# Forming the weight sums of a seven-product block scheme on GpSimd instead of VectorE

## Chip, cores, metric

One core of one Trainium2 chip. The time is that of the device, in microseconds (us), of one execution; lower is better. The engines are PE (TensorE matmul) with PEld (its weight loads), DVE (VectorE), ACT (ScalarE), POOL (GpSimd) and SP (SyncE). In the profile a line such as L331 is a line of the kernel. SBUF and PSUM are the two on-chip memories: in this kernel the results of PE's products lie in PSUM, and weights, activations and sums in SBUF.

## The reference

A gated recurrence over 4 sequences of 6080 steps and 256 channels, then a two-layer block with `h - tanh(h)` between its layers (256 to 2048 to 256), on the 24320 resulting rows, all in float32. Shortened:

```python
sig = 1.0 / (1.0 + np.exp(-f_logit))
f = lower_bound + (1.0 - lower_bound) * sig
for t in range(S):
    h = f[:, t] * h + (1 - f[:, t]) * x[:, t]
    y[:, t] = h
...
h = x @ w_in                 # x: y as 24320 rows
g = h - np.tanh(h)
return (g @ w_out).astype(np.float32)
```

## The kernel before

The rows go through in 48 blocks: one of 256 rows, then 47 of 512. From the third block on, both matrix products use a scheme with seven block products in place of eight (Winograd's form of Strassen's). It needs, for each of the four parts of `w_in` and of `w_out`, three sums S1, S2, S4 of weight blocks, and a difference S3, which takes the place of block A21. The sums are formed once and then serve all blocks. The first two blocks are computed plainly (eight products) while the weights, which arrive as 64-bit numbers, are still being rounded to float32 on DVE and ACT.

```python
w_in  = [wpool.tile([P, 7, 2 * P], FP32, name=f"w_in{u}")  for u in range(NU)]   # NU = 4
w_out = [wpool.tile([P, 7, 2 * P], FP32, name=f"w_out{u}") for u in range(NU)]
A11, S3, A12, A22, S1, S2, S4 = range(7)
...
def sum_weight(kind, u, s3):
    w = (w_in, w_out)[kind][u]
    A21 = S3
    sums = (
        (S1, A21, A22, ALU.add),
        (S2, S1, A11, ALU.subtract),
        (S4, A12, S2, ALU.subtract),
    )
    for o, a, b, op in ((S3, A11, A21, ALU.subtract),) if s3 else sums:
        nc.vector.tensor_tensor(
            out=w[:, o, :], in0=w[:, a, :], in1=w[:, b, :], op=op
        )
```

The order of instructions is fixed by hand in a list of words, one queue per engine. `cw.i` is the last step of rounding a weight (L132), `sc` the recurrence (L231, a scan), `F` a plain product of the first layer (L687), `S` one of the second (L754), `A.k.u` the three sums of part u of `w_in` (k=0) or `w_out` (k=1), `B.k.u` its difference. `K1` are filler matmuls.

```python
before = """
    ... cw.1 sc0.1 ... sc1.1 cr.2 K1.2 ... F.1.0.0 ... F.1.0.1 ... cw.2 ... F.0.1.0 ...
    cw.3 ... S.0.0.0 ... cw.4 ... F.0.2.0 ...
    q.0.3.0 A.0.0 F.1.3.0 ... cw.7 ... B.0.0 ... A.0.1 ... B.0.1 ... cw.8 ... A.0.3 ... A.1.3 ... A.0.2 ...
"""
```

## Time and profile before

| | before |
|---|---|
| median of 3 runs | 2330.94 us (2330.39 to 2331.64) |
| PE busy of the 2330.1 us span | 2318.8 us |
| DVE busy | 2121.3 us |
| POOL busy | 0.7 us |
| the 32 sums, on DVE | between 67 and 131 us |

The prediction below shows the page's lines and reads them.

```profile
18.16 0.67 DVE L725 SCALAR_TENSOR_TENSOR q<-q,t 128x512 f32<-128x512 f32 x1
18.75 0.69 DVE L138 TENSOR_SCALAR e<-raw 128x1024 int32<-128x1024 int32 x1
...
30.96 1.43 DVE L132 SCALAR_TENSOR_TENSOR w_out<-r,e 128x256 f32<-128x256 f32 x4
```

### The profile page before, as it was taken

How to read it: one execution, taken by the hardware profiler on the slowest of the kernel's cores; microseconds unless marked ns; L12 is line 12 of the kernel's file. 1: busy time of each engine (PE TensorE's matmuls, PEld its weight loads, DVE VectorE, ACT ScalarE, POOL GpSimd, SP SyncE). 2: the span in 40 equal slices, each digit the busy share in tenths (PEclk: the TensorE clock that was granted, in tenths of full speed). 3: DMA queues.
4: the chain of work that ended last, by engine and by line, in shares of the span. 5: the costliest groups of instructions: out<-in, count | busy, mean ns of one | idle time of the engine just before them, and what ended most of it. 6: DMA issues, size and time to landing. Idle time of an engine off the chain costs nothing.

```text
span 2330.1 us, 28649 instructions
## 1 busy us (share of the span) xinstructions
PE 2318.8 (100%) x10676; PEld 2025.3 (87%) x10676; DVE 2121.3 (91%) x2447; ACT 1800.6 (77%) x2686; POOL 0.7 (0%) x6
## 2 busy tenths in 40 slices
PE   9999999999999999999999999999999999999998
PEld 5888888888888888888888888888888888888887
DVE  8999899998999989999899999999899998999987
ACT  7777777777777777787777777777777777777775
POOL 0000000000000000000000000000000000000000
PEclk9999999999999999999999999999999999999999
DMA  6311211112111111111111121111211112111101
GB/s 172 64 23 29 45 37 28 28 33 41 37 28 28 37 37 37 28 28 40 33 37 28 28 44 30 37 28 28 46 28 37 28 28 46 31 33 28 28 10 29
DMA packets 296948, 85.05 MB, mean 36 GB/s; under 512 B 289888, under 2 KB 292704, under 8 KB 296800
## 3 DMA queue, kind: packets, MB, share of 16 engines
q1 hardware_dynamic: 296512, 82.87, 16.9%
q8 instruction: 85, 1.39, 0.3%
q14 instruction: 63, 0.52, 0.1%
q10 hardware_dynamic: 288, 0.26, 0.0%
HBM read 58.20 MB, written 24.90 MB: 36 GB/s over the span
## 4 chain that ended last, share of the span: by engine, by line
PE 99%; DMA 0%; DVE 0%; issue 0%; ACT 0%; SPq 0%
PE A L388 27%; PE Qd L471 14%; PE Qa L471 14%; PE D L388 14%; PE Qb L471 14%; PE B L388 7%; PE Qc L471 7%; PE A L687 1%; PE Qc L754 1%; PE Qa L754 1%; PE Qb L754 1%; PE D L687 0%; PE Qd L687 0%; PE B L687 0%; DMA fn<-in_f_logit_dram 0%; PE Qa L687 0%
## 5 line engine op out<-in xcount | busy, mean ns | idle before, releaser
L388 PE MATMUL A<-T,w_in 128*128 128x256 f32 x2208 | 558.8, 379 | 0.0
L388 PEld LDWEIGHTS A<-T,w_in 128*128 128x128 f32 x2208 | 419.5, 190 | 57.0
L432 DVE TENSOR_TENSOR h<-h,q 128x1024 f32<-128x1024 f32 x368 | 437.6, 1220 | 3.1
L426 DVE SCALAR_TENSOR_TENSOR q<-q,t 128x1024 f32<-128x1024 f32 x368 | 440.0, 1216 | 0.0
L419 ACT ACTIVATE q<-t 128x1024 f32<-128x1024 f32 x368 | 382.8, 1053 | 46.7 <-DVE h L432 43.8
L416 ACT ACTIVATE t<-h 128x1024 f32<-128x1024 f32 x368 | 388.6, 1056 | 3.1 <-DVE h L403 0.3
L437 ACT ACTIVATE junk<-t 128x1024 bf16<-128x1024 f32 x368 | 388.1, 1055 | 1.5
L451 DVE TENSOR_TENSOR Tg<-h 128x1024 f32<-128x1024 f32 x368 | 348.0, 946 | 6.4
L471 PE MATMUL Qb<-h,w_out 128*128 128x256 f32 x1472 | 347.7, 379 | 0.0
L471 PEld LDWEIGHTS Qb<-h,w_out 128*128 128x128 f32 x1472 | 279.7, 190 | 38.0
L471 PE MATMUL Qd<-h,w_out 128*128 128x256 f32 x736 | 219.0, 379 | 0.0
L471 PE MATMUL Qa<-Tg,w_out 128*128 128x256 f32 x736 | 219.0, 379 | 0.0
L471 PE MATMUL Qa<-h,w_out 128*128 128x256 f32 x736 | 218.9, 379 | 0.0
L471 PE MATMUL Qd<-Tg,w_out 128*128 128x256 f32 x736 | 218.9, 379 | 0.0
L400 ACT COPY h<-B 128x512 f32<-128x512 f32 x184 | 106.9, 581 | 143.0 <-PE B L388 94.2
L400 ACT COPY h<-A 128x512 f32<-128x512 f32 x184 | 107.2, 583 | 136.7 <-PE A L388 125.3
L403 DVE TENSOR_TENSOR h<-D,r 128x512 f32<-128x512 f32 x184 | 126.9, 689 | 92.7 <-PE D L388 89.1
L403 DVE TENSOR_TENSOR h<-A,r 128x512 f32<-128x512 f32 x184 | 126.3, 687 | 73.8 <-PE A L388 42.1
L400 ACT COPY r<-A 128x512 f32<-128x512 f32 x184 | 107.2, 583 | 105.9 <-PE A L388 105.9
L388 PE MATMUL D<-T,w_in 128*128 128x256 f32 x736 | 188.9, 379 | 0.0
L388 PE MATMUL A<-y,w_in 128*128 128x256 f32 x736 | 188.9, 379 | 0.0
L388 PE MATMUL B<-y,w_in 128*128 128x256 f32 x736 | 188.9, 379 | 0.0
(120 smaller groups left out, 3069.2 us busy)
## 6 DMA issues: line engine op xcount, KB each, us to landing
xn<-in_x_dram SPq DMA_DIRECT2D x184, 128.0 KB, 3.3
fn<-in_f_logit_dram SPq DMA_DIRECT2D x184, 128.0 KB, 3.1
out_dram<-osb SPq DMA_DIRECT2D x180, 128.0 KB, 2.8
raw<-in_moe_w_out_dram SPq DMA_DIRECT2D x8, 512.0 KB, 4.9
raw<-in_moe_w_in_dram SPq DMA_DIRECT2D x7, 512.0 KB, 4.7
out_dram<-osb SPq DMA_DIRECT2D x3, 256.0 KB, 3.9
fn<-in_f_logit_dram SPq DMA_DIRECT2D x1, 512.0 KB, 7.3
xn<-in_x_dram SPq DMA_DIRECT2D x1, 512.0 KB, 8.2
```

Of the source, the lines that this page charges most:

```text
L388: nc.tensor.matmul(ps[:, c], lhsT=w_in[u][:, slot, c * P : (c + 1) * P], rhs=mixes[j][right], start=start and c == 0, stop=True, skip_grou ...
L400: nc.scalar.copy(out=dst, in_=piece(n, bank))
L403: nc.vector.tensor_tensor(out=piece(n, "h")[:, q], in0=piece(n, bank), in1=piece(n, r), op=ALU.add)
L416: nc.scalar.activation(out=half(n, i, "t"), in_=half(n, i), func=AF.Square)
L419: nc.scalar.activation(out=half(n, i, "q"), in_=half(n, i, "t"), func=AF.Square, scale=RA, bias=RB,)
L426: nc.vector.scalar_tensor_tensor(out=q, in0=q, scalar=RC, in1=t, op0=ALU.add, op1=ALU.mult)
L432: nc.vector.tensor_tensor(out=h, in0=h, in1=q, op=ALU.mult)
L437: nc.scalar.activation(out=junk[:, :, :, 0 : st[n]["hb"]], in_=t, func=AF.Relu, bias=-TINY, accum_out=flags[:, 2 * n + i : 2 * n + i + 1],)
L451: nc.vector.tensor_tensor(out=o, in0=a, in1=b, op=ALU.subtract)
L471: nc.tensor.matmul(acc[j, part][:, r, 0 : st[n]["hb"]], lhsT=w_out[u][:, slot, c * P : (c + 1) * P], rhs=piece(n, right)[:, q, c], start=( ...
L687: nc.tensor.matmul(h[c], lhsT=w_in[u][:, 2 * k + s, c * P : (c + 1) * P], rhs=ys[j][:, k, 0:nb], start=k == 0 and (c == 0 or len(banks) == 2),
L754: nc.tensor.matmul(acc[j][i // 2][:, i % 2].rearrange("p (k m) -> p k m", k=2), lhsT=plain[j, u][:, s, c, i * P : (i + 1) * P], rhs=w_out[ ...
```

## The change

The intent: DVE is 91% busy and GpSimd idle, so the sums of the weights move to GpSimd, in the same order.

```diff
@@ -328,7 +328,7 @@
             for o, a, b, op in ((S3, A11, A21, ALU.subtract),) if s3 else sums:
-                nc.vector.tensor_tensor(
+                nc.gpsimd.tensor_tensor(
                     out=w[:, o, :], in0=w[:, a, :], in1=w[:, b, :], op=op
                 )
```

## The prediction

> **What bounds the kernel now.** I read four views in this order. First the page of the profile: busy time by engine, and the chain that ended last.
>
> ```profile
> PE 2318.8 (100%) x10676; PEld 2025.3 (87%) x10676; DVE 2121.3 (91%) x2447; ACT 1800.6 (77%) x2686; POOL 0.7 (0%) x6
> ...
> PE 99%; DMA 0%; DVE 0%; issue 0%; ACT 0%; SPq 0%
> ```
>
> PE (TensorE) is busy 2318.8 of 2330.1 us and the chain that ended last is PE for 99%; GpSimd (POOL) is empty. Next the busy time in stretches that I chose round the changed work.
>
> ```profile
> core 0: us, PE busy (x) PEld busy (x) DVE busy (x) ACT busy (x) POOL busy (x), PEclk, DMA share, GB/s
> 0.00:20.00 20.00, 14.76 (x60) 9.65 (x61) 13.11 (x24) 11.73 (x23) 0.70 (x6) 0.91 0.98 268
> 20.00:67.00 47.00, 47.00 (x174) 32.85 (x173) 46.45 (x63) 37.80 (x60) 0.00 (x0) 1.00 0.42 121
> 67.00:131.00 64.00, 64.00 (x282) 53.24 (x282) 58.62 (x94) 46.69 (x76) 0.00 (x0) 1.00 0.24 46
> ...
> 200.00:2200.00 2000.00, 2000.00 (x9269) 1760.61 (x9268) 1830.99 (x2076) 1560.67 (x2317) 0.00 (x0) 1.00 0.16 33
> 2200.00:2331.00 131.00, 123.99 (x578) 108.39 (x576) 108.33 (x124) 89.96 (x134) 0.00 (x0) 0.99 0.07 17
> ```
>
> All of PE's idle time lies in the first 20 us (5.2) and the last stretch (7.0). From 20 us on it has no hole. DVE (VectorE) is also nearly full from 20 to 67 us, 46.45 of 47. Third, the changed line by itself.
>
> ```profile
> L331 DVE TENSOR_TENSOR w_in<-w_in x16: 389/424/430, 67.3 to 119.1; 128x256 f32<-128x256 f32 x16
> L331 DVE TENSOR_TENSOR w_out<-w_out x16: 416/422/427, 97.4 to 130.2; 128x256 f32<-128x256 f32 x16
> ```
>
> There are 32 of them in the whole kernel, all between 67 and 131 us, where PE waits for nothing. Last, the timelines of DVE and PE in the opening (columns: start, length, then the work), for how close DVE runs ahead of PE.
>
> ```profile
> 15.19 0.68 DVE L132 SCALAR_TENSOR_TENSOR w_in<-r,e 128x512 f32<-128x512 f32 x1
> 15.79 2.45 DVE L231 TENSOR_TENSOR_SCAN y<-f,y,v 128x512 f32<-128x512 f32 x2
> ...
> 23.42 1.22 DVE L132 SCALAR_TENSOR_TENSOR w_in<-r,e 128x1024 f32<-128x1024 f32 x1
> ...
> 40.52 1.22 DVE L132 SCALAR_TENSOR_TENSOR w_in<-r,e 128x1024 f32<-128x1024 f32 x1
> ```
>
> ```profile
> 18.39 0.59 PE L858 MATMUL B<-zeros 128*128 128x512 bf16 x2
> 18.82 1.88 PE L687 MATMUL Qa<-y,w_in 128*128 128x512 f32 x4
> ...
> 25.69 1.89 PE L687 MATMUL B<-y,w_in 128*128 128x256 f32 x8
> ...
> 42.91 1.89 PE L687 MATMUL D<-y,w_in 128*128 128x256 f32 x8
> ```
>
> The scans end at 18.24 and PE uses their y at 18.82, after filler matmuls: 0.6 us of slack. The second weight block is rounded by 24.64 and used at 25.69: 1.05 us. The third is ready at 41.74 and used at 42.91: 1.2 us. These are DVE's tightest dates; bank releases and second-layer weights have 2 us and more.
>
> **What the Trainium skill says.** "GPSIMD Engine Reference", section 3.1, gives a two-input tensor_tensor as about 2.6 cycles an element, 4497 ns for 2048 fp32 columns, about twice VectorE. No GpSimd tensor_tensor is in this trace to compare; the DVE rows here, 424 ns for 256 columns, 688 for 512 and 1220 for 1024, are about 1.04 ns an element, consistent with its VectorE figure (2293 ns). "SBUF — State Buffer", section "Who interferes with whom": a VectorE instruction with two SBUF inputs, or in a two-port mode, and a GpSimd instruction that reads SBUF exclude each other for a whole instruction, the later one waiting. The trace before can't show it, having no such GpSimd work. "Perfetto Trace Analysis", section "Optimizing Scalar/DVE Operations", warns for that reason that moving work between the two "might not help".
>
> **The change part by part.**
> *Removed from DVE:* eight groups of three dependent sums and eight single differences. In the timeline a triple takes 1.25 us of queue (67.29 to 68.54) and a single 0.34 (82.07 to 82.41): 8 x 1.25 + 8 x 0.34 = 12.7 us, all after 67 us. None is on the path that sets the end, since PE has no hole there. Worth: 0.
>
> *Added to GpSimd:* 32 instructions of 256 columns. Estimate from the page's 4497 ns: 4497 x 256 / 2048 = 0.56 us, plus dispatch, say 0.65 us; within a triple each waits for the one before, say 0.2 us more. In all some 32 x 0.85 = 27 us of an empty engine, spread over about 110 us. PE needs them in time: the first (S1 of the first block) at 89.7 us, the last group at 140 to 157. Enough.
>
> *Moved:* order is kept per engine, but GpSimd has nothing ahead of the sums, so each now starts when its operands are ready instead of in its place in DVE's queue. By the instruction order built from the changed kernel, the first triple waits only for the rounding that ends at 15.87 us, so it runs from 16 us instead of 67; the first difference waits for PE's plain products of that block (about 25.7 us); the second triple for the rounding at 24.64; its difference for PE at about 43 us; the triple of the fourth block for the rounding at 60.8. So eight GpSimd sums land between 16 and 45 us, where DVE has no slack time and its results are used within 0.6 to 1.2 us. The other 21 come after the last rounding (96.2 us), where DVE is relieved of its sums and starts with two transposes and waits for PE.
>
> *What that costs if the page's lock is as it says and the two alternate* (each sum holds DVE up for its 0.65 us unless DVE is on an instruction with a PSUM input). First sum asked for at 16.1, granted at 17.0 between the scans: y late by 0.65 against 0.6 of slack, PE loses about 0.1 to 0.2. Three sums before the second rounding: 3 x 0.65 = 1.95 late less 1.05 of slack: PE is 0.9 to 1.1 behind. Three more (a difference, two sums; the last sum of that triple falls beside a PSUM read) before the third rounding: 6 x 0.65 = 3.9 less 1.2, so PE is about 2.7 behind. After that the dates have 2 us and more of their own beyond this 2.7, and DVE's lead grows by the 12.7 us removed. A delay of PE is never recovered, since it has no idle to give back: about +2.7 us on 2330.9, that is 2333.6.
>
> **The rivals.**
> 1. *Nothing moves.* DVE keeps the port by issuing back to back, and GpSimd fits into PSUM reads (one at 19.95 us, others at 26.9, 29.8, 30.4, 34.0), or the two overlap better than the page says. For: dates for the sums are 45 us off in the early part. Against: the measured lock of the page. Time: 2330.9.
> 2. *GpSimd becomes late itself.* After 96.2 us nine sums lie between the third block's triple and the first second-layer difference, needed at 119.0 us. With each waiting for a 1.2 us DVE instruction, 9 x 1.85 = 17 us from about 101 to 118. Close, but DVE also has holes there (1.2 us at 126 already before). If missed, 1 to 3 us more: 2334 to 2337.
> 3. *Faster, because DVE is relieved at 91% busy.* Against: the sums are not in the 2000 us of steady work at all, and PE has no hole where they were. It could be tenths at most.
>
> **Range and chances.** I give the lock with alternation about half, nothing about 40%, late sums 10%. Between 2330.9 and 2333.6 I choose 2332.5. The low end is the lowest of before; the high end adds 0.9 us a sum instead of 0.65 in the early part (6 x 0.9 - 1.2 = +4.2 and some lateness). Two per cent is 47 us, which nothing here reaches: same 0.985, faster 0.005, slower 0.01.
>
> **What would show it right or wrong.** In the changed kernel's trace: 32 sums on POOL with starts at 16 to 20, 25 to 45, and after 60 us; a start-to-start spacing of 0.7 to 1 us in an undisturbed triple; the second scan, the second rounding and the third rounding later than 18.24, 24.64 and 41.74 by 0.65, 2 and 4 us if the lock holds, unchanged if not; PE holes before the matmuls that stood at 25.69 and 42.91 and nowhere else, of about 1 and 1.7 us; from 200 to 2200 us PE still full. The prediction is wrong if PE waits for POOL anywhere, if a sum on POOL takes well over 1 us, or if the time falls below 2330.

## More of the kernel before

```profile
32.57 3.62 PE L754 MATMUL Qa<-w_out,h 128*128 128x256 f32 x16
```

The columns are start, length (both us), engine, line, operation, what it writes and reads, shapes and count. The four pieces of the rounding start 0.33 us apart; the product reads the first two, done by 31.7, and starts at 32.57.

## The result

| | median, us | runs, us |
|---|---|---|
| before | 2331.29 | 2330.39 to 2331.98 (4) |
| changed | 2332.36 | 2331.95 to 2332.43 (4) |

The ratio is 1.0003, 95% interval 0.9988 to 1.0018: the same within 2%. A ratio here is the mean time of one kernel's fast runs over that of the other's fast runs of the same rounds, so it is not quite the ratio of the medians.

The page and the stretches of the changed kernel, in the forms shown of before:

```profile
PE 2319.1 (100%) x10674; PEld 2024.9 (87%) x10676; DVE 2117.5 (91%) x2415; ACT 1801.5 (77%) x2686; POOL 43.7 (2%) x38
...
PE 98%; DVE 1%; DMA 0%; issue 0%; SPq 0%; ACT 0%; DVEq 0%
```

```profile
20.00:67.00 47.00, 45.47 (x169) 31.56 (x168) 46.84 (x62) 38.33 (x60) 14.63 (x8) 1.00 0.39 120
67.00:131.00 64.00, 63.95 (x281) 53.26 (x281) 53.63 (x63) 46.23 (x75) 24.10 (x21) 1.00 0.23 46
...
200.00:2200.00 2000.00, 2000.00 (x9268) 1760.62 (x9267) 1830.50 (x2076) 1561.18 (x2316) 0.00 (x0) 1.00 0.16 33
```

DVE has 32 instructions fewer and POOL 32 more. The steady 2000 us are untouched. PE lost 1.53 us between 20 and 67 us, where it had no hole before, and DVE now has a share in the chain that ended last. The sums by themselves, and GpSimd's timeline:

```profile
L331 POOL TENSOR_TENSOR w_in<-w_in x16: 730/1056/4455, 15.0 to 117.8; 128x256 f32<-128x256 f32 x16
```

```profile
15.00 4.37 POOL L331 TENSOR_TENSOR w_in<-w_in 128x256 f32<-128x256 f32 x3 [13.69 <-DVE w_in L132]
23.65 9.00 POOL L331 TENSOR_TENSOR w_in<-w_in 128x256 f32<-128x256 f32 x4 [4.28 <-PE Qd L687]
42.88 2.41 POOL L331 TENSOR_TENSOR w_in<-w_in 128x256 f32<-128x256 f32 x1 [10.23 <-PE B L687]
61.43 3.54 POOL L331 TENSOR_TENSOR w_in<-w_in 128x256 f32<-128x256 f32 x3 [16.14 <-DVE w_in L132]
96.87 2.35 POOL L331 TENSOR_TENSOR w_out<-w_out 128x256 f32<-128x256 f32 x3 [31.90 <-DVE w_out L132]
...
102.17 15.64 POOL L331 TENSOR_TENSOR w_out<-w_out 128x256 f32<-128x256 f32 x11
```

The brackets tell what ended the idle time before a group. The first eleven sums start as soon as a rounding (DVE), a plain product (PE) or the sum before them lets them, from 15 us on; on DVE the first had started at 67.3. A sum takes 0.73 us where it is alone (96.87 to 99.22: three in 2.35 us) and up to 4.46 us where DVE is at work. The profile's lengths on GpSimd are rough, so the readings that follow rest on DVE and PE. What that does to DVE and PE:

```profile
14.84 2.88 DVE L231 TENSOR_TENSOR_SCAN y<-f,y,v 128x512 f32<-128x512 f32 x2
17.64 1.15 DVE L725 SCALAR_TENSOR_TENSOR q<-q,t 128x512 f32<-128x512 f32 x1
18.71 1.21 DVE L138 TENSOR_SCALAR e<-raw 128x1024 int32<-128x1024 int32 x1
...
23.93 1.25 DVE L132 SCALAR_TENSOR_TENSOR w_in<-r,e 128x1024 f32<-128x1024 f32 x1
...
31.47 2.13 DVE L132 SCALAR_TENSOR_TENSOR w_out<-r,e 128x256 f32<-128x256 f32 x4
```

```profile
17.39 1.88 PE L687 MATMUL Qa<-y,w_in 128*128 128x512 f32 x4
...
25.32 1.96 PE L687 MATMUL B<-y,w_in 128*128 128x256 f32 x8 [0.89 <-DVE w_in L132]
...
33.08 3.69 PE L754 MATMUL Qa<-w_out,h 128*128 128x256 f32 x16 [0.64 <-DVE w_out L132]
```

Against before, the two scans take 2.88 us instead of 2.45, L725 1.15 instead of 0.67, L138 1.21 instead of 0.69: 0.43 to 0.52 us more for each of the first three sums. The second rounding so ends 10.34 us after the first scan's start, where it took 8.85 before, and PE waits 0.89 us for it. The four pieces of the first `w_out` rounding take 2.13 us instead of 1.43, and PE waits 0.64 us more. PE never waits for POOL.

**A measure that leaves the start out.** The spans differ by only 0.5 us (2330.1 and 2330.6), because in this trace the changed kernel came out of its start earlier: its first 512-column plain product stands at 17.39 us, that of before at 18.82. In the trace of before the granted clock is 0.91 over the first 20 us (half speed for 3.4 us), in the changed one's 1.00. So below I use the *PE stretch*: from the start of that product to the start of the last second-layer product that reads h, near the end. It is 2303.20 us before and 2305.10 changed: +1.90. The two holes of 0.89 and 0.64 are this: a matmul's recorded length (379 ns) overlaps the next, which starts 216 ns after it, so each reported hole is some 0.16 us short, and 0.89 + 0.64 + 2 x 0.16 = 1.85. Below, a *hole* is the reported one; the loss is 0.16 more.

### The profile page after: what moved, and what is told of

It is laid out like the page before. It is cut to its first block, busy times and chain, and to the rows that moved or that the text cites. A ratio compares the mean times of both kernels' runs of the same rounds, so it can differ in the third digit from the quotient of the medians.

```text
span 2330.6 us, 28656 instructions
## 1 busy us (share of the span) xinstructions
PE 2319.1 (100%) x10674; PEld 2024.9 (87%) x10676; DVE 2117.5 (91%) x2415; ACT 1801.5 (77%) x2686; POOL 43.7 (2%) x38
## 3 DMA queue, kind: packets, MB, share of 16 engines
q8 instruction: 85, 1.39, 0.3%
## 4 chain that ended last, share of the span: by engine, by line
PE 98%; DVE 1%; DMA 0%; issue 0%; SPq 0%; ACT 0%; DVEq 0%
PE A L388 27%; PE Qd L471 14%; PE Qb L471 14%; PE Qa L471 14%; PE D L388 14%; PE B L388 7%; PE Qc L471 7%; PE Qa L754 1%; PE Qb L754 1%; PE Qc L754 1%; DMA xn<-in_x_dram 0%; PE D L687 0%; PE Qd L687 0%; PE A L687 0%; PE B L687 0%
## 5 line engine op out<-in xcount | busy, mean ns | idle before, releaser
L388 PE MATMUL D<-y,w_in 128*128 128x256 f32 x736 | 188.9, 379 | 0.0
```

The costliest lines, as they stand in the source:

```text
L388: nc.tensor.matmul(ps[:, c], lhsT=w_in[u][:, slot, c * P : (c + 1) * P], rhs=mixes[j][right], start=start and c == 0, stop=True, skip_grou ...
```

## The experiments

**Theory:** the early start of the sums is the cost. Eight of them now run where DVE is full and PE close behind it; each that reads SBUF holds up a DVE instruction at the read port that they share, and DVE's lateness reaches PE. **Rivals:** (1) the difference is only luck of the start; (2) sums on GpSimd cost wherever they are, or come too late for PE; (3) it is not the reading, but any GpSimd instruction in that place; (4) there was something to win on DVE, and the cost hides it.

| run | stretch, us | holes in PE (16 to 60 us), us | clock, first product to the 512-column one, us |
|---|---|---|---|
| before, first trace | 2303.20 | none | half for a while, 5.26 |
| before, again | 2303.20 | none | full from 13.6 us, 4.78 |
| changed, first trace | 2305.10 | 0.89, 0.64 | full, 4.75 |
| changed, again | 2305.99 | 1.39, 1.02 | full, 4.75 |
| gated to 70 us | 2303.09 | none | full from 14.3 us, 4.92 |
| early eight on DVE | 2303.09 | none | full, 4.75 |
| only the early eight on GpSimd | 2304.66 | 0.34, 0.64 | half, 5.31 |
| early sums twice | 2307.05 | 1.78, 1.70 | half, 5.50 |
| no sums | 2303.09 | none | half, 5.42 |
| write-only, too soon | 2303.09 | none | half, 5.84 |
| write-only, in place | 2303.28 | none reported | full, 4.75 |
| one-input copies | 2304.00 | 0.58 | full, 4.75 |

Both kernels have two traces, every other run one. No hole under 0.15 us is reported. In "before, again" and "gated" the record of the clock begins only after the first product, at the time given. Some expectations count from the 512-column product to the end of the span instead; the part after the stretch takes 7.75 to 8.69 us in these traces, so the stretch is the finer measure. To the end it was 2311.29 us before and 2311.52 again, 2313.25 and 2313.98 changed, 2311.50 gated, 2311.03 write-only.

**Both kernels again.** No edit.

> The kernel before, unchanged, profiled and timed again to learn how far the opening differs from run to run. Theory (the sums on GpSimd hold DVE up in the opening): no PE hole between 16 and 2200 us, and from the first 512-column plain product (18.82 us in the first trace) to the end of the span 2311.3 us again, whatever the start does. Rival (the 1 us between the kernels is luck of the start): that stretch itself differs by a us or more between the two traces of this same kernel.

> The changed kernel, unchanged, profiled and timed again. Theory: PE holes of about 0.9 us before the first product of the second weight block and 0.6 us before the first second-layer product come back, DVE instructions beside an early sum are again about 0.5 us longer, and from the first 512-column plain product to the end it takes 2313.2 us, 2 us over before; timed +1 to +2 us. Rival (luck of the start): the holes do not come back, or the time is within 0.3 us of before.

Measured: before 2330.29 us (2329.90 to 2331.68, 5 runs), ratio 0.9994 to the shared runs of before, 2331.36 (2330.37 to 2332.37, 9 runs); changed 2333.32 us (2332.43 to 2334.27, 5 runs), ratio 1.0008 (0.9994 to 1.0021). The stretch of before is the same to 0.01 us in both traces, so rival 1 falls: the timed runs scatter by 2 us, and in the twelve traces the 512-column product stands anywhere from 16.85 to 19.48 us, but the stretch of before does not move, and the holes come back. They are larger here: sums that waited in the first trace got the port in this one. The second trace of before also shows how near DVE is to PE when the start has a full clock, on DVE and then on PE:

```profile
23.45 1.23 DVE L132 SCALAR_TENSOR_TENSOR w_in<-r,e 128x1024 f32<-128x1024 f32 x1
```

```profile
25.24 1.89 PE L687 MATMUL B<-y,w_in 128*128 128x256 f32 x8
```

The second block is rounded by 24.68 and used at 25.24: 0.56 us, where the first trace had 1.05. A PE that has to wait starts 0.14 us after the rounding's end (25.18 to 25.32 in the changed kernel's first trace), so 0.42 us of it is slack.

The DVE timeline of the changed kernel's second trace, then its PE timeline:

```profile
24.09 1.74 DVE L132 SCALAR_TENSOR_TENSOR w_in<-r,e 128x1024 f32<-128x1024 f32 x1
```

```profile
25.97 1.97 PE L687 MATMUL B<-y,w_in 128*128 128x256 f32 x8 [1.39 <-DVE w_in L132]
...
34.12 2.18 PE L754 MATMUL Qa<-w_out,h 128*128 128x256 f32 x9 [1.02 <-DVE w_out L132]
```

In the first trace the rounding at this place took 1.25 us and the sum that had asked for the port 0.3 us earlier took 4.46 us; here the same sum took 0.95 us and the rounding 1.74. Who got the port there differed between two runs of one kernel.

**Gated: all sums on GpSimd, but none before 70 us.**

```diff
+    gate = const.tile([P, 1], FP32, name="gate")
...
+            if (kind, u, s3) == (0, 0, False):
+                nc.gpsimd.tensor_copy(
+                    out=gate[:], in_=p_temp(0, 3, 0, "t")[:, 0, 0:1]
+                )
```

> All sums stay on GpSimd, but a copy of one column of a late activation (ready at about 70 us) stands ahead of the first, so none starts before 70 us. Theory (the early start is the cost): no hole in PE between 16 and 200 us, DVE stretched only after 70 us, stretch from the first 512-column plain product to the end 2311.3 us, timed equal to before within 0.4 us. Rival 1 (any sum on GpSimd costs, by contention late as early): +1 us or more remains, with PE holes after 70 us. Rival 2 (GpSimd late for PE): a PE hole of a us or more before a product that reads a sum, between 89 and 125 us.

Measured: 2330.52 us (2330.26 to 2332.19, 5 runs), ratio 0.9997 (0.9983 to 1.0010). That is 0.84 us under the median of before, more than the 0.4 I had allowed and within its scatter (before itself, again, came out 1.07 under). GpSimd's timeline of the gated kernel:

```profile
69.71 0.18 POOL L327 COPY gate<-t 128x1 f32<-128x1 f32 x1 [68.39 <-ACT t L717]
69.85 9.79 POOL L336 TENSOR_TENSOR w_in<-w_in 128x256 f32<-128x256 f32 x11
```

The sums that cost PE 2 us now run from 70 to 80 us and cost it nothing. They still hold DVE up (the two L210 instructions of before's 1.41 us, here L211, take 2.21), but there DVE is well ahead of PE. Rival 2 falls with this run. The stretch is 0.11 us shorter than before's: in the trace of before one second-layer matmul at 138.5 us starts 0.11 us late, and here it does not. That is all that DVE's relief brought.

**The early eight back on DVE, and the early eight alone on GpSimd.**

```diff
-                nc.gpsimd.tensor_tensor(
+                (nc.vector if kind == 0 and u < 2 else nc.gpsimd).tensor_tensor(
```

> The eight sums of the first two blocks of the first weight stay on DVE in their old places; the other 24 go to GpSimd. Theory (only the early eight cost): no PE hole between 16 and 60 us, equal to before within 0.4 us. Rival (the later 24 cost the difference): +1 us remains.

> Only the eight sums of the first two blocks of the first weight go to GpSimd; the other 24 stay on DVE. Theory (the early eight are the whole cost): PE holes of 0.9 to 1.4 us before the second weight block's first product and 0.6 to 1.0 us before the first second-layer product, as with all 32; from the first 512-column plain product to the end 2313.2 to 2314.0 us. Rival (the cost needs the other 24 too): 2311.4 us as before.

The second run has the two engines exchanged in that line. Measured: early eight on DVE 2331.14 us (2329.59 to 2332.04, 5 runs), ratio 0.9998; early eight alone on GpSimd 2333.39 us (2332.11 to 2334.21, 4 runs) against 2330.52, ratio 1.0009 (0.9992 to 1.0026). The 24 later sums on GpSimd cost nothing and the eight early ones alone bring the holes. The stretch to the end of the span came out at 2312.84 us, under my 2313.2 to 2314.0: the first hole was 0.34 us. DVE was as late there (the rounding ended 10.30 us after the scan's start), but PE too, by 0.56 us (5.31 - 4.75 in the table), in a start with a half clock: the slack is not a constant.

**The early sums twice.**

```diff
+            if kind == 0 and u < 2 and not s3:
+                sums = sums + sums
```

> As the changed kernel, with the six early S1, S2, S4 sums of the first two blocks made twice on GpSimd, the same values again. Theory (each early sum that meets a DVE instruction with two SBUF inputs holds it up by about 0.5 us): three more before the second rounding, so the hole there grows by about 1.5 us, to 2.4 to 2.9 us; the three of the second block fall after it and add up to 1.5 us at a later date if they are not starved; stretch to the end 2315 to 2317 us. Rival (what costs is the start of GpSimd, or a wait, once, not each sum): 2313.2 to 2314.0 us as in the changed kernel.

Measured: 2335.34 us (2334.27 to 2336.29, 4 runs), ratio 1.0018 (1.0001 to 1.0034); to the end of the span 2315.74 us, within the range. The rounding ends 11.91 us after the scan's start, 3.06 later than before for six sums met, 0.51 each, so the cost goes by the sum. The hole there was 1.78 us, not 2.4 to 2.9: again PE started late with a half clock (0.75 us).

**Write-only instructions in place of the early sums.** Wrong results, here and in the next two; the slower fallback is kept off by raising `TINY`.

```diff
+            if kind == 0 and u < 2:
+                for o in (S3,) if s3 else (S1, S2, S4):
+                    for _ in range(3):
+                        nc.gpsimd.memset(w[:, o, :], 0.0)
+                return
```

> Wrong result on purpose: each of the eight early sums is replaced by three GpSimd memsets of the same 128x256 slot, which write and read nothing (the check that would start the slower fallback is switched off by its threshold). Theory (the shared read port is what is fought over): the DVE scans and the rounding keep their lengths of before (1.23 and 1.22 us), no PE hole between 16 and 60 us, stretch to the end 2311.4 us. Rival (any GpSimd instruction in that place costs, by its writes to SBUF or by its semaphores): DVE instructions stretched by tenths of a us and a hole before the second weight block's first product.

Measured: 2330.54 us (2329.83 to 2332.07, 4 runs) against 2330.52, no hole. But the first nine memsets, having no operand to wait for, ran long before the scans, so the run tells little of them. I made it again with each triple behind a GpSimd copy of one column of its weight:

```diff
+                if not s3:
+                    nc.gpsimd.tensor_copy(out=gate[:], in_=w[:, 3, 255:256])
```

> Wrong result on purpose. As the write-only run, whose first nine memsets had no operand to wait for and ran far too soon, but each of the two triples now stands behind a GpSimd copy of one column of the weight it used to read, so that the memsets run beside the two scans and the second rounding as the sums did. Theory (the shared read port): scans, 2x-mode and rounding instructions keep their lengths of before within 0.1 us (scans 2.45 us for both, rounding 1.22), no PE hole, first 512-column product to the last second-layer product 2303.1 us. Rival (GpSimd work of any kind in that place costs): scans 2.6 us or more, a hole before the second weight block.

Measured: 2330.14 us (2329.96 to 2331.36, 4 runs) against 2331.51, ratio 0.9995. Timelines of this run, DVE and then GpSimd:

```profile
14.72 2.45 DVE L232 TENSOR_TENSOR_SCAN y<-f,y,v 128x512 f32<-128x512 f32 x2
17.09 0.67 DVE L733 SCALAR_TENSOR_TENSOR q<-q,t 128x512 f32<-128x512 f32 x1
17.68 0.82 DVE L139 TENSOR_SCALAR e<-raw 128x1024 int32<-128x1024 int32 x1
18.42 0.87 DVE L150 TENSOR_SCALAR m<-raw 128x1024 int32<-128x1024 int32 x1
```

```profile
15.92 4.00 POOL L336 MEMSET w_in<- 128x256 f32 x9
```

Nine memsets run beside the scans and L725's like (here L733), and these keep their lengths of before, 2.45 and 0.67 us. Rival 3 falls for instructions with two SBUF inputs: what they fight over is reading. The two integer instructions with one input, which do 1024 columns in 0.69 us alone, were stretched to 0.82 and 0.87, more than the 0.1 us I had allowed. That makes DVE 0.34 us late, and a little of it does reach PE, at the first second-layer product:

```profile
31.14 3.69 PE L762 MATMUL Qa<-w_out,h 128*128 128x256 f32 x16
```

It starts 0.11 us after PE was free, and the stretch is 0.18 us longer than that of the runs without a hole.

**One-input copies in place of the early sums.**

```diff
+            if kind == 0 and u < 2:
+                for o, a, b, op in ((S3, A11, A21, ALU.subtract),) if s3 else sums:
+                    nc.gpsimd.tensor_copy(out=w[:, o, :], in_=w[:, a, :])
+                return
```

> Wrong result on purpose: each of the eight early sums is a GpSimd copy of its first operand alone (128x256, one input). Theory (any GpSimd read takes the port, for as long as it reads): DVE instructions that meet one are again stretched, but by less than the 0.4 to 0.5 us of a sum, about 0.1 to 0.3 us each, as a copy is shorter; PE hole before the second weight block's first product under 0.9 us or none; first 512-column product to the last second-layer product 2303.1 to 2304.5 us. Rival (it takes two operands on GpSimd to collide): no stretch and 2303.1 us.

Measured: 2331.51 us (2331.02 to 2332.17, 4 runs) against 2331.51, ratio 1.0001. Two lines, DVE and then PE (L729 is L725 here):

```profile
16.76 0.81 DVE L729 SCALAR_TENSOR_TENSOR q<-q,t 128x512 f32<-128x512 f32 x1
```

```profile
31.43 3.69 PE L758 MATMUL Qa<-w_out,h 128*128 128x256 f32 x16 [0.58 <-DVE w_out L132]
```

DVE is stretched by 0.09 us in the scans, 0.14 in L725 and 0.19 in L138: one operand read by GpSimd is enough, and it costs less than two (0.43 to 0.52). The second rounding was 0.44 us late, and no hole stood before the second weight block; one of 0.58 us stood before the first second-layer product. The runs show that GpSimd has to read for a two-input instruction to be held up; that it is a shared port, and nothing else that two readers share, is the skill's word (cited in the prediction) and not shown.

**No sums at all.**

```diff
+            return
...
-                    lhsT=w_in[u][:, slot, c * P : (c + 1) * P],
+                    lhsT=w_in[u][:, slot % 4, c * P : (c + 1) * P],
...
-                        lhsT=w_out[u][:, slot, c * P : (c + 1) * P],
+                        lhsT=w_out[u][:, slot % 4, c * P : (c + 1) * P],
```

> Wrong result on purpose: no sums at all, on any engine; the products that would read a sum read a plain block in its place (fallback switched off as well). Theory (on DVE the sums are covered by PE): no gain, stretch to the end 2311.4 us, PE without a hole, DVE with some 12.7 us more idle time between 67 and 131 us. Rival (the sums on DVE cost something that the change could have won): under 2310.5 us.

Measured: 2330.86 us (2329.66 to 2332.12, 4 runs) against 2330.52, ratio 0.9998; to the end 2311.17 us. The stretches of this run:

```profile
20.00:67.00 47.00, 47.00 (x174) 32.77 (x173) 46.30 (x62) 37.78 (x60) 0.00 (x0) 1.00 0.41 121
67.00:131.00 64.00, 63.95 (x282) 53.24 (x282) 47.63 (x62) 46.63 (x76) 0.00 (x0) 1.00 0.23 46
```

DVE is busy 47.63 us between 67 and 131 us instead of 58.62, PE 63.95 of 64.00, and the time is that of before. (That is 11.0 us less, for 12.7 expected; over the span DVE is busy 2109.3 us, 12.0 less than before. In the changed kernel it fell by only 3.8, as the stretched instructions took the rest.) Rival 4 falls: there was nothing to win by taking the sums off DVE, wherever they go. For the same reason no run here beats the kernel before; the gated one equals it.

## Why the prediction was right

The time fell inside the range, 2332.36 us for a predicted 2332.5, and 2333.32 when timed again. By its steps:

1. *PE is the bound and the removed 12.7 us are worth 0.* Right: without any sums the stretch is 0.11 us shorter, and that is one late matmul. (So PE did have that small hole after 20 us, which the prediction denies; and 0.9 of its 7.0 us at the end lie beyond the span of 2330.1.)
2. *The sums start when their operands are ready, eight of them between 16 and 45 us.* Right, to a us: 15.0 to 42.9.
3. *A sum takes 0.65 us, 0.85 from start to start.* Measured 0.73 and 0.81 undisturbed. Right enough.
4. *Each early sum holds DVE up by 0.65 us.* The mechanism was right and the size too large: 0.43 to 0.54 us. The second rounding was 1.49 us late, not 1.95, and 1.99 in the second trace, in which the following difference got in front of it.
5. *PE loses 0.1 to 0.2 us at the scans.* It lost nothing there. The kernel issues that product as two matmuls, each two of the x4 records, and only the second reads the second scan's y. It starts 0.86 us after the first, at 19.68 us in before, so the slack was 1.4 us and not 0.6 (1.0 with a full clock, in the second trace). The scan was 0.43 late.
6. *About 1 us before the second weight block, at 1.05 us of slack.* Holes of 0.89 and 1.39 us, losses of 1.05 and 1.55. That the first agrees is luck: two errors cancel. DVE's lateness was taken too large (step 4) and so was the slack, which had been read from a trace with a half clock in its start; with a full clock PE comes sooner, and the slack was 0.44 us in both traces (1.49 - 1.05 and 1.99 - 1.55; 0.42 by the second trace of before). The copies fit it: 0.44 us late, no hole.
7. *About 1.7 us before the third weight block; "bank releases and second-layer weights have 2 us and more".* This step failed. There was no hole there. The date that I missed is the first second-layer product, whose weights were ready 0.85 us ahead, and 0.4 with a full clock (31.76 for 32.13 us in the second trace of before); PE's holes there were 0.64 and 1.02 us, its second loss. By then PE was itself late enough for the third block, whose rounding came 2.2 us late (3.1 in the second trace), not 3.9.
8. *The sums alternate with DVE.* Only in part. In the first trace two sums waited 4.46 and 2.90 us while DVE ran on; in the second the same sums got in. What decides it stays open. Later they do alternate: from 103.8 us on, six of seven sums take 1.6 to 1.7 us each, and DVE's 1024-column instructions beside them 1.56 to 1.75 us instead of 1.22.
9. *Nine sums from about 101 to 118, in 17 us, needed at 119.* They ran from 101.5 to 113.2 and PE never waited for POOL, so rival 2 did not come about.

The sum was +2.7 us if the lock held; the stretch shows +1.9 and +2.8. The 2332.5 was an average with the case of no effect, so its closeness owes something to the start, which moves a timed run by 2 us.

## What to carry to other kernels

Moving work to an idle engine gains only where the engine that it leaves sets a date of the bound one; here PE had no hole where the work was. An instruction moved in an in-order queue is also moved in time: in an empty queue it starts as soon as its operands are ready, which may be just where the engine it shares a port with is tight, and a one-column copy that waits for something late is enough to hold it back. To see 2 us of effect under 2 us of scatter, measure between two instructions of the bound engine, not the whole span.

## What the Trainium skill lacked or had wrong

- "GPSIMD Engine Reference", section 3.1, gives 4497 ns for a tensor_tensor of 2048 columns, and no small size of it. A 128x256 float32 tensor_tensor took 0.73 us alone and 0.81 us from start to start when each waits for the one before; scaling the page's figure by columns gives 0.56 (an estimate), so some 0.17 us or more do not scale.
- "SBUF — State Buffer", section "Who interferes with whom", is borne out in what collides: two-input DVE instructions were stretched by GpSimd sums (0.67 to 1.15 us) and by copies (to 0.81), not by memsets (0.67), while one-input integer instructions at double rate (1024 columns in 0.69 us, for 1.22 with two inputs) were stretched by memsets (to 0.82 and 0.87), as it says of the two-port modes; that these instructions are in one is inferred from their rate. It lacks the size: 0.43 to 0.54 us of DVE time for a sum of 0.73 us.
- The same section says, of DVE's two-port modes, that whoever issues first gets the shared pair and the other blocks, and in general that issue order decides. Here a sum that began to wait behind such an integer instruction (L149, until 24.04 us) was passed by three later DVE instructions with two SBUF inputs and took 4.46 us; in another run of the same kernel the same sum took 0.95 us.
